# The first pair of an attention-and-FFN kernel worked by halves of heads, with another order of steps and loads

## The chip, the cores and the metric

The kernel runs on one core of one Trainium2 chip. The metric is the device time of one execution in microseconds, given as the median of several runs. The core's engines work side by side, each through its own queue in order: TensorE (products), VectorE, ScalarE, GpSimd (here almost only an issuer of loads) and SyncE (here an issuer of moves and stores). A trace of one profiled execution shows what each engine did and what it waited for.

## The reference

Attention in chunks of 64 tokens over 8 heads of 64, then a feed-forward part in which two products of the same input are multiplied element by element. Nothing stands between the last two weights, so the kernel multiplies them into one.

```python
# q, k, v: (8 batches, 8 heads, 576 tokens, 64), float32; chunks of 64 tokens
scores = scale * np.matmul(q_c, k_c.transpose(0, 1, 2, 4, 3))
scores = scores - np.max(scores, axis=-1, keepdims=True)
attn = np.exp(scores)
attn = attn / (np.sum(attn, axis=-1, keepdims=True) + 1e-09)
x = np.matmul(attn, v_c)          # then all heads side by side: (4608 tokens, 512)
a = x @ w1                        # w1, w2: (512, 1024)
b = x @ w2
out = (a * b @ w3) @ w_out        # w3: (1024, 1024), w_out: (1024, 512)
```

## The kernel before

The 4608 tokens are cut into 18 pairs of 256 tokens (four chunks, all heads). Two pairs make a group of 512 tokens. Every engine's work is written out by hand in one string, `ORDER`: a letter for the kind of step, then its pair (or group) and part. A loop calls the functions in that order, and `inorder` keeps each engine's instructions in the order of the string. So each engine, and GpSimd's queue of loads, works through its own letters of the string from left to right, and an instruction that waits holds up all that stands behind it on its engine.

The steps of pair p, with the line that the trace names:

- `R0`, `R1` load q and k of pair 0 as float32 by the queues of SyncE and ScalarE (L139); `K0`, `K1` cast them to bfloat16 on ScalarE (L145).
- `q`, `k`, `v` load the other pairs through GpSimd, which casts on the way (L99). `i0` to `i3` load a quarter of w1 and of w2 each, `o` loads w_out in four pieces, `h0` and `h1` load half of w3 in four pieces each. At most eight loads of GpSimd are under way: each further one waits for the landing of the one eight before it.
- `T p.0`, `T p.1` transpose q and k in blocks on VectorE (L205). `S p` is the scores on TensorE (L96), `E p` the exponential on ScalarE (L238), `P p` the product with v, which carries a column of ones for the sums (L96).
- `N p.0`, `N p.1` divide by the sums on VectorE (L266 and L269), `X p.0`, `X p.1` transpose the result into the input of the feed-forward part (L302, from pair 6 on L310).
- From pair 6 on, blocks are moved between partitions by DMAs of SyncE: `G` (four DMAs for each half) between T and S, `H` between X and A.
- `A p.j` and `B p.j` are x*w1 and x*w2 for a slice of the 1024 columns (L96; eight products of 256 columns up to pair 3, four products of 512 columns by groups after that). `C` copies A's result on ScalarE (L367), `M` multiplies it with B's on VectorE (L384).
- `V`, `W`, `Z` form w3*w_out once: transposes on VectorE (L425), products on TensorE, copies on ScalarE (L438).
- `O p` is the last product, 16 products of 512 columns (L96), `Y p` its copy on ScalarE (L414), `Q p` its store by SyncE.
- `D` are products of zeros on TensorE, into a PSUM tile that the next step will use: `D which.p.j.n.columns`.

PSUM is one pool of four tiles (two banks each) for scores, values, A with B, W and O. A tile comes free when its reader is through: E for scores, N for values, M for A and B, Z for W, Y for O. Tiles for q and k are five, for v six, for transposed q and k two (of a group each).

At the start TensorE runs 92 products of zeros with 16 columns and 8 with 512, then S0, P0, S1, five more products of zeros, and then the first x*w1, `A0.0`. Around `O0`, the first output product, the order before has `W3`, then `P4` and `S5`, then `O0`.

Of the kernel before, what the change touches and what calls it, by code (L numbers as in the profile page):

```python
# [24 lines left out]
G6.1 N10.1 C8.0 M6.7 M8.0 X10.0 X10.1 k15 P11 A8.1 A8.2 B8.1 N11.0 B8.2 k16 A8.3 C8.1 C8.2 N11.1
X11.0 B8.3 A8.4 M8.1 v13 B8.4 S12 C8.3 M8.2 S13 C8.4 H5.0 X11.1 M8.3 A8.5 E12 A8.6 C8.5 M8.4 B8.5
C8.6 T15.0 H5.1 B8.6 A8.7 B8.7 T15.1 M8.5 E13 P12 M8.6 A10.0 T16.0 B10.0 N12.0 C8.7 A10.1 N12.1 M8.7
P13 C10.0 v14 M10.0 C10.1 B10.1 N13.0 N13.1 A10.2 M10.1 X12.0 A10.3 B10.2 X12.1 C10.2 C10.3 q17
A10.4 M10.2 B10.3 x12 G7.0 B10.4 X13.0 G7.1 C10.4 A10.5 v15 k17 M10.3 X13.1 M10.4 x11 A10.6 S14 S15
T16.1 T17.0 T17.1 B10.5 C10.5 B10.6 C10.6 E14 O6 M10.5 Q5 M10.6 E15 P14 N14.0 N14.1 G8.0 Y6 X14.0 O7  # L30
# [17 lines left out]
def first_path(  # L48
# [46 lines left out]
    def mm(*a, **kw):
        return inorder(nc.tensor.matmul(*a, **kw))  # L96
# [34 lines left out]
    qk_t = {}  # L131

    HH = H // 2
    raw_t = {}
# [4 lines left out]
        inorder((nc.sync, nc.scalar)[s].dma_start(  # L139
            raw_t[s][:], (q, k)[s][0, :, 0:4 * CH, :].rearrange("h (p t) d -> p h (t d)", t=2)))  # L140

    def do_K(s):
# [2 lines left out]
        inorder(nc.scalar.copy(qk_t[0][:, s], raw_t[s][:]))  # L145
# [88 lines left out]

    def do_E(p, hh=None):
        if p not in e_t:
            e_t[p] = asb.tile([P, 2, H, CH], bf, tag="e", bufs=2, name="e")
        inorder(nc.scalar.activation(  # L238
            e_t[p][:, :, heads(hh)], s_t[p][:].rearrange("p u (h q) -> p u h q", q=CH)[:, :, heads(hh)],
            Exp, scale=scale, bias=0.0))  # L240
# [345 lines left out]
```

## Time and profile before

| | |
|---|---|
| median of 3 runs | 243.89 us (243.85 to 244.39) |
| profiled execution | 244.65 us, of it 243.1 from the first to the last instruction |
| TensorE busy | 229.1 us, 94% |
| VectorE, ScalarE, GpSimd busy | 152.9, 84.1, 83.9 us |
| mean granted TensorE clock | 0.985 |
| loads through GpSimd | 18.88 MB, 83.4% of the DMA engines' time |

A row of a timeline gives the start in microseconds from the span's start, the time that the row covers, the engine, the line, the operation with its output and inputs, how many instructions are merged, and in brackets the idle time of the engine before it with what ended it. A row of the table by stretches gives the stretch, its length, the busy time and instruction count of TensorE, of its weight load, of VectorE, ScalarE and GpSimd, then the granted clock, the mean number of tenths or share in which the DMA engines were busy, and GB/s. In the page's row of slices each digit is one fortieth of the span (6.1 us), in tenths. Ends of products are modelled, so a wait inside a group of products can hide in its busy time.

### The profile page before, as it was taken

The page shows a single profiled execution, that of the slowest core. Times are in us where ns is not written, and L with a number is a line of the kernel's source. Part 1 is how long each engine was busy: PE and PEld are TensorE (multiplying, and loading weights), DVE is VectorE, ACT ScalarE, POOL GpSimd, SP SyncE. Part 2 cuts the span into 40 slices and gives each one's busy share as a digit, 9 for nine tenths or more (in the row PEclk, how much of TensorE's full clock was granted, in tenths as well). Part 3 has the DMA queues.
Part 4 walks back from the last instruction along what each step waited for, and adds up shares of the span by engine and source line. Part 5 has one row for each costly group of instructions (what it writes and reads, how often), then busy time and mean ns, then how long its engine had stood idle before and what let it go on. Part 6 is the DMA issues. An engine that isn't in the chain of part 4 may idle for free.

```text
span 243.1 us, 6370 instructions
## 1 busy us (share of the span) xinstructions
PE 229.1 (94%) x2685; PEld 121.6 (50%) x2705; DVE 152.9 (63%) x235; ACT 84.1 (35%) x116; POOL 83.9 (35%) x114
## 2 busy tenths in 40 slices
PE   7479899999999899999999999999999999999994
PEld 5248778854545444443434444444444444444443
DVE  1678798789888598959878899663843422321200
ACT  2513423314422625333533435253224125323122
POOL 7757966656953353642920082000000000000000
PEclk9859999999999999999999999999999999999999
DMA  6999999999999999999999799647302142003234
GB/s 172 179 185 182 184 169 199 197 193 174 172 187 288 221 214 262 212 219 189 192 275 202 183 191 130 142 119 246 105 1 88 44 131 86 0 0 114 86 149 173
DMA packets 94366, 39.23 MB, mean 161 GB/s; under 512 B 75264, under 2 KB 86784, under 8 KB 94336
## 3 DMA queue, kind: packets, MB, share of 16 engines
q0 software_dynamic: 82592, 18.88, 83.4%
q1 hardware_dynamic: 10704, 19.41, 26.8%
q10 hardware_dynamic: 1040, 0.52, 0.8%
q8 instruction: 21, 0.34, 0.6%
q14 instruction: 9, 0.07, 0.1%
HBM read 38.80 MB, written 9.44 MB: 198 GB/s over the span
## 4 chain that ended last, share of the span: by engine, by line
PE 45%; DMA 41%; POOL 6%; DVE 3%; issue 3%; SPq 0%; POOLq 0%; DVEq 0%
PE ab_ps L96 27%; PE o_ps L96 17%; DMA qk<-in_k_dram 16%; DMA vbuf<-in_v_dram 12%; DMA w<-in_moe_w_dram 8%; DMA qkm<-qkT 3%; DMA xt<-xm 3%; POOL qk L99 2%; POOL vbuf L99 2%; POOL w L99 1%; DVE qkT L205 1%; POOL wo L99 1%; DVE xn L269 1%; PE pv L96 1%; DVE xm L310 1%
## 5 line engine op out<-in xcount | busy, mean ns | idle before, releaser
L96 PE MATMUL ab_ps<-xt,w 128*128 128x512 bf16 (+1 forms) x684 | 128.0, 342 | 2.2 <-DMA w<-in_moe_w_dram 0.6
L96 PEld LDWEIGHTS <-w 128*128 128x128 bf16 x704 | 67.0, 98 | 57.0 <-issue 2.3
L384 DVE TENSOR_TENSOR ab<-a_sb,ab_ps 128x512 bf16<-128x512 f32 x71 | 46.7, 674 | 47.2 <-PE ab_ps L96 40.4
L96 PE MATMUL o_ps<-w3o,ab 128*128 128x512 bf16 (+1 forms) x284 | 64.0, 373 | 0.8 <-DVE ab L384 0.2
L367 ACT COPY a_sb<-ab_ps 128x512 f32<-128x512 f32 x71 | 41.4, 588 | 67.0 <-PE ab_ps L96 61.5
L205 DVE STREAM_TRANSPOSE qkT<-qk 128x1024 bf16<-128x1024 bf16 x36 | 45.9, 1298 | 13.2 <-ACT qk L145 5.5
L96 PEld LDWEIGHTS <-ab 128*128 128x128 bf16 x296 | 28.5, 98 | 32.5 <-issue 0.2
L99 POOL DMA_DIRECT2D vbuf<-in_v_dram x40 | 33.9, 852 | 17.1 <-DMA qk<-in_k_dram 7.4
L414 ACT COPY o_sb<-o_ps 128x1024 f32<-128x1024 f32 x17 | 17.2, 1013 | 53.9 <-PE o_ps L96 44.4
L269 DVE TENSOR_TENSOR xn<-pv,rcs 128x512 bf16<-128x512 f32 x36 | 24.9, 691 | 1.3
L99 POOL DMA_DIRECT2D qk<-in_q_dram x23 | 18.1, 788 | 15.0 <-DMA qk<-in_q_dram 5.3
L238 ACT ACTIVATE e<-s_ps 128x1024 bf16<-128x1024 f32 x17 | 17.1, 1025 | 13.0 <-PE s_ps L96 12.8
L99 POOL DMA_DIRECT2D qk<-in_k_dram x23 | 18.1, 789 | 8.8 <-DMA vbuf<-in_v_dram 4.9
L310 DVE STREAM_TRANSPOSE xm<-xn 128x512 bf16<-128x512 bf16 x24 | 16.0, 689 | 0.1
L96 PE MATMUL w_ps<-wo,w3T 128*128 128x512 bf16 x62 | 13.9, 379 | 0.1
L266 DVE RECIPROCAL rcs<-pv 128x8 f32<-128x8 f32 x36 | 6.9, 192 | 10.6 <-PE pv L96 10.6
L99 POOL DMA_DIRECT2D w<-in_moe_w_dram x16 | 11.1, 696 | 5.5 <-DMA wo<-in_moe_w_out_dram 2.3
L96 PEld LDWEIGHTS <-e 64*32 64x32 bf16 (+1 forms) x768 | 7.6, 99 | 8.2 <-issue 5.1
L96 PE MATMUL pv<-vbuf,e 64*32 64x65 bf16 (+1 forms) x768 | 10.0, 198 | 1.7 <-ACT e L238 1.1
L425 DVE STREAM_TRANSPOSE w3T<-w 128x1024 bf16<-128x1024 bf16 x8 | 9.4, 1214 | 1.8 <-DMA w<-in_moe_w_dram 1.6
L96 PEld LDWEIGHTS <-w3T 128*128 128x128 bf16 x64 | 6.3, 98 | 7.3
L96 PE MATMUL z_ps<-zero 128*128 128x16 bf16 (+1 forms) x103 | 7.8, 222 | 1.9 <-DVE zero L115 1.4
(29 smaller groups left out, 48.9 us busy)
## 6 DMA issues: line engine op xcount, KB each, us to landing
out_dram<-o_sb SPq DMA_DIRECT2D x17, 512.0 KB, 3.4
qkm<-qkT SPq DMA_DIRECT2D x48, 128.0 KB, 6.5
vbuf<-in_v_dram POOLq DMA_DIRECT2D x32, 128.0 KB, 8.3
w<-in_moe_w_dram POOLq DMA_DIRECT2D x16, 256.0 KB, 9.5
xt<-xm SPq DMA_DIRECT2D x48, 64.0 KB, 3.7
qk<-in_q_dram POOLq DMA_DIRECT2D x11, 256.0 KB, 9.5
qk<-in_k_dram POOLq DMA_DIRECT2D x11, 256.0 KB, 10.6
wo<-in_moe_w_out_dram POOLq DMA_DIRECT2D x4, 256.0 KB, 7.1
```

The lines of the kernel that those rows point to most:

```text
L96: return inorder(nc.tensor.matmul(*a, **kw))
L99: return inorder(nc.gpsimd.dma_start(dst, src))
L205: inorder(nc.vector.transpose(qkT_t[g][:, :, p % 2, s, heads(h)].rearrange("p e h (y t) -> p h t e y", t=2), qk_t[p][:, s, heads(h)].rearr ...
L238: inorder(nc.scalar.activation(e_t[p][:, :, heads(hh)], s_t[p][:].rearrange("p u (h q) -> p u h q", q=CH)[:, :, heads(hh)], Exp, scale=sca ...
L266: inorder(nc.vector.reciprocal(rc, pv[:, :, :, D:W]))
L269: inorder(nc.vector.tensor_mul(xn_t[p][:, u], pv[:, :, :, 0:D], rc.to_broadcast([P, 2, 4, D])))
L310: inorder(nc.vector.transpose(xm_t[g][:, u, :, m].rearrange("p o (c y) -> p c o y", y=BL), xn_t[p][:].rearrange("p u r m d -> p (u r) m d" ...
L367: first[p, j] = inorder(nc.scalar.copy(a_t[p, j][:], ps_t[p, j][:, 0, :]))
L384: inorder(nc.vector.tensor_mul(o, view(a_t.pop((p, j))[:]), view(ps_t.pop((p, j))[:, 1, :])))
L414: inorder(nc.scalar.copy(o_sb[:], ps_t.pop(p)[:]))
L425: inorder(nc.vector.transpose(w3T_t[f][:].rearrange("p k (f y) -> p f k y", y=BL), w3[:, NB * f:NB * (f + 1), :].rearrange("p f (k x) -> p ...
```

## The change

`K`, `T`, `S`, `E` and `P` of pair 0 are each called twice, for heads 0 to 3 and 4 to 7. `K` learns to do half, and the scores of the two halves go to two PSUM tiles, so the first exponential need not wait for the second half's scores. The 92 small and 8 large products of zeros at the start become 16 large ones; six new ones stand in front of S1, and the five behind it become six. The whole string is in another order, for the steps and for the loads.

```diff
-R0 R1 v0 q1 k1 i0 v1 i1 i2 q2 k2 v2 i3 q3 k3 v3 q4 k4 v4 o h0 h1 D0.0.0.92.16 D0.0.0.8.512 K0 T0.0
-K1 T0.1 q5 k5 v5 S0 T1.0 E0 P0 T1.1 q6 k6 v6 N0.0 S1 D1.0.0.5.512 X0.0 N0.1 X0.1 A0.0 E1 B0.0 C0.0
...
-v7 V0 B3.2 C3.2 V1 A3.3 M3.2 S4 B3.3 W0 k9 C3.3 V2 V3 W1 Z0 V4 V5 T5.0 V6 V7 W2 Z1 W3 M3.3 T5.1 q10
-T6.0 E4 T6.1 Z2 P4 T7.0 S5 T7.1 N4.0 Z3 k10 O0 T8.0 O1 q11 E5 N4.1 X4.0 Y0 G3.0 q12 X4.1 Y1 k11 P5
-v8 N5.0 N5.1 O2 Q0 X5.0 X5.1 G3.1 A4.0 O3 T8.1 C4.0 Y2 S6 E6 S7 T9.0 T9.1 Q1 B4.0 T10.0 M4.0 A4.1
-G4.0 T10.1 E7 P6 Y3 B4.1 v9 N6.0 C4.1 N6.1 A4.2 G4.1 C4.2 B4.2 M4.1 X6.0 M4.2 A4.3 P7 q13 q14 N7.0
-Q2 B4.3 C4.3 A4.4 N7.1 k12 B4.4 M4.3 A4.5 X6.1 C4.4 C4.5 B4.5 A4.6 k13 k14 C4.6 M4.4 A4.7 S8 T11.0
-v10 B4.6 B4.7 M4.5 q15 X7.0 X7.1 M4.6 C4.7 S9 M4.7 E8 P8 N8.0 O4 E9 N8.1 Q3 P9 Y4 H3.0 O5 T11.1 X8.0
-T12.0 H3.1 v11 T12.1 Y5 N9.0 T13.0 A6.0 G5.0 B6.0 N9.1 X8.1 C6.0 X9.0 A6.1 C6.1 B6.1 T13.1 A6.2 B6.2
...
+R0 R1 v0 K0.0 T0.0.0 K0.1 K1.0 D0.0.1.16.512 T0.0.1 q1 K1.1 k1 T0.1.0 S0.0 T0.1.1 T1.0 S0.1 E0.0 i0
+E0.1 P0.0 P0.1 D0.1.0.6.512 N0.0 T1.1 S1 D1.0.0.6.512 E1 v1 i1 i2 N0.1 q2 X0.0 X0.1 k2 A0.0 P1 i3
+N1.0 v2 N1.1 B0.0 X1.0 X1.1 A0.1 C0.0 B0.1 C0.1 v3 A0.2 A1.0 M0.0 M0.1 B0.2 T2.0 B1.0 C0.2 C1.0 T2.1
...
+A1.3 X2.1 o B1.3 A2.0 T3.0 C1.2 C1.3 B2.0 T3.1 M1.2 C2.0 M1.3 q5 M2.0 S3 E3 A2.1 B2.1 C2.1 h1 T4.0
+q6 P3 A2.2 M2.1 q7 N3.0 N3.1 B2.2 A2.3 X3.0 C2.2 X3.1 C2.3 B2.3 T4.1 V0 A3.0 B3.0 M2.2 k5 C3.0 k6
+M2.3 V1 V2 A3.1 M3.0 k7 C3.1 B3.1 M3.1 V3 A3.2 T5.0 B3.2 W0 S4 Z0 V4 v4 V5 W1 V6 W2 E4 C3.2 Z1 V7 W3
+T5.1 Z2 q8 A3.3 T6.0 T6.1 T7.0 B3.3 T7.1 v5 Z3 M3.2 S5 C3.3 k8 M3.3 E5 T8.0 G3.0 O0 P4 N4.0 O1 q9
+N4.1 X4.0 q10 Y0 T8.1 G3.1 P5 X4.1 k9 N5.0 Y1 O2 Q0 X5.0 v6 S6 N5.1 X5.1 T9.0 T9.1 v7 S7 A4.0 Q1
+B4.0 E6 E7 O3 C4.0 M4.0 P6 N6.0 Y2 k10 N6.1 A4.1 C4.1 q11 v8 B4.1 G4.0 A4.2 Y3 C4.2 P7 v9 B4.2 M4.1
+k11 X6.0 X6.1 N7.0 A4.3 B4.3 N7.1 A4.4 A4.5 M4.2 T10.0 C4.3 G4.1 q12 B4.4 A4.6 M4.3 k12 C4.4 X7.0 Q2
+Q3 M4.4 H3.0 C4.5 S8 E8 T10.1 B4.5 X7.1 C4.6 M4.5 H3.1 B4.6 A4.7 M4.6 B4.7 C4.7 M4.7 P8 S9 E9 T11.0
+N8.0 O4 T11.1 Y4 O5 q13 N8.1 v10 T12.0 X8.0 X8.1 P9 A6.0 C6.0 N9.0 N9.1 T12.1 Y5 B6.0 A6.1 B6.1 C6.1
...
-    def do_K(s):
+    def do_K(s, h=None):
         if 0 not in qk_t:
             qk_t[0] = io.tile([P, 2, H, 2 * D], bf, tag="qk", bufs=5, name="qk")
-        inorder(nc.scalar.copy(qk_t[0][:, s], raw_t[s][:]))
+        inorder(nc.scalar.copy(qk_t[0][:, s, heads(h)], raw_t[s][:, heads(h)]))
...
     def do_S(p, hh=None):
         g, m = divmod(p, 2)
-        if p not in s_t:
-            s_t[p] = psum("s_ps")
+        if (p, hh) not in s_t:
+            s_t[p, hh] = psum("s_ps")
...
     def do_P(p, hh=None):
         e = e_t[p]
-        vb_free.append(vb_t[p])
+        if hh != 0:
+            vb_free.append(vb_t[p])
...
-        d, key = ((s_t, p), (ps_t, (p, j)), (pv_t, (p, 0)))[which]
+        d, key = ((s_t, (p, (None, 0)[j])), (ps_t, (p, j)), (pv_t, (p, 0)))[which]
```

More of the change, by code (lines that the diff above doesn't have):

```diff
@@ L25 @@
[L25 to L30, printed above, removed]
@@ new lines @@
+N8.0 O4 T11.1 Y4 O5 q13 N8.1 v10 T12.0 X8.0 X8.1 P9 A6.0 C6.0 N9.0 N9.1 T12.1 Y5 B6.0 A6.1 B6.1 C6.1
+A6.2 X9.0 B6.2 A6.3 G5.0 X9.1 M6.0 B6.3 A6.4 C6.2 B6.4 M6.1 G5.1 C6.3 T13.0 M6.2 k13 H4.0 A6.5 M6.3
+C6.4 q14 C6.5 S10 B6.5 v11 A6.6 H4.1 T13.1 E10 M6.4 P10 M6.5 S11 C6.6 B6.6 G6.0 N10.0 G6.1 q15 N10.1
+k14 A6.7 v12 M6.6 X10.0 E11 P11 B6.7 A8.0 N11.0 k15 C6.7 B8.0 A8.1 C8.0 q16 k16 X10.1 M6.7 N11.1
+B8.1 T14.0 A8.2 C8.1 A8.3 B8.2 C8.2 M8.0 M8.1 B8.3 X11.0 Q4 S12 S13 C8.3 M8.2 v13 X11.1 T14.1 H5.0
@@ new lines @@
+A8.4 E12 C8.4 B8.4 M8.3 A8.5 E13 P12 M8.4 N12.0 A8.6 C8.5 B8.5 q17 N12.1 A8.7 C8.6 M8.5 T15.0 k17
+x12 T15.1 B8.6 X12.0 B8.7 T16.0 v14 O6 C8.7 T16.1 M8.6 v15 H5.1 A10.0 M8.7 Y6 B10.0 Q5 C10.0 A10.1
+C10.1 M10.0 P13 N13.0 G7.0 A10.2 T17.0 B10.1 B10.2 v16 C10.2 x11 N13.1 A10.3 A10.4 C10.3 B10.3 M10.1
+A10.5 T17.1 C10.4 G7.1 M10.2 B10.4 B10.5 S14 M10.3 C10.5 G8.0 M10.4 X12.1 X13.0 G8.1 E14 S15 H6.0
+X13.1 O7 M10.5 P14 N14.0 E15 A10.6 N14.1 Y7 B10.6 A10.7 C10.6 Q6 M10.6 P15 N15.0 C10.7 S16 N15.1
+X14.0 B10.7 H6.1 M10.7 O8 A12.0 X14.1 E16 B12.0 C12.0 A12.1 Q7 Y8 X15.0 X15.1 P16 v17 M12.0 S17
@@ new lines @@
+N16.0 B12.1 H7.0 A12.2 C12.1 B12.2 M12.1 E17 C12.2 P17 N16.1 H7.1 A12.3 B12.3 N17.0 M12.2 A12.4
+B12.4 A12.5 C12.3 B12.5 M12.3 N17.1 C12.4 A12.6 X16.0 M12.4 C12.5 A12.7 C12.6 B12.6 M12.5 A14.0
+C12.7 Q8 O9 M12.6 A14.1 Y9 B12.7 C14.0 B14.0 M12.7 B14.1 A14.2 C14.1 B14.2 A14.3 X16.1 M14.0 C14.2
+M14.1 A14.4 B14.3 X17.0 C14.3 O10 Y10 M14.2 A14.5 M14.3 C14.4 A14.6 C14.5 B14.4 B14.5 C14.6 B14.6
+H8.0 A14.7 Q9 M14.4 O11 Q10 B14.7 Y11 X17.1 H8.1 C14.7 M14.5 M14.6 A16.0 A16.1 A16.2 M14.7 C16.0
+B16.0 Q11 M16.0 B16.1 A16.3 O12 C16.1 C16.2 Y12 B16.2 M16.1 A16.4 B16.3 A16.5 M16.2 C16.3 C16.4
@@ L40 @@
+B16.4 B16.5 O13 M16.3 C16.5 M16.4 A16.6 Q12 A16.7 Y13 Q13 M16.5 B16.6 O14 C16.6 B16.7 M16.6 C16.7
+O15 M16.7 Y14 Q14 O16 Y15 Q15 Y16 Q16 O17
 """
@@ L140, in do_R, with heads @@
             raw_t[s][:], (q, k)[s][0, :, 0:4 * CH, :].rearrange("h (p t) d -> p h (t d)", t=2)))
-    def do_K(s):
+    def heads(h):
+        return slice(0, H) if h is None else slice(h * HH, (h + 1) * HH)
+    def do_K(s, h=None):
         if 0 not in qk_t:
             qk_t[0] = io.tile([P, 2, H, 2 * D], bf, tag="qk", bufs=5, name="qk")
-        inorder(nc.scalar.copy(qk_t[0][:, s], raw_t[s][:]))
-    def heads(h):
-        return slice(0, H) if h is None else slice(h * HH, (h + 1) * HH)
+        inorder(nc.scalar.copy(qk_t[0][:, s, heads(h)], raw_t[s][:, heads(h)]))
     def load_qk(p, which, h=None):
@@ L225, in do_S @@
                     for i in range(NB):
-                        mm(s_t[p][half[i % 2], i // 2, h * CH:(h + 1) * CH],
+                        mm(s_t[p, hh][half[i % 2], i // 2, h * CH:(h + 1) * CH],
                            lhsT=qkT_t[g][blk[i], e, m, 1, h, :], rhs=qkT_t[g][blk[i], e, m, 0, h, :],
@@ L230, in do_S @@
                 for i in (0, 3, 1, 2):
-                    mm(s_t[p][half[i % 2], i // 2, h * CH:(h + 1) * CH],
+                    mm(s_t[p, hh][half[i % 2], i // 2, h * CH:(h + 1) * CH],
                        lhsT=qkm_t[g][half[i // 2], i % 2, m, 1, h, :],
@@ L238, in do_E @@
         inorder(nc.scalar.activation(
-            e_t[p][:, :, heads(hh)], s_t[p][:].rearrange("p u (h q) -> p u h q", q=CH)[:, :, heads(hh)],
+            e_t[p][:, :, heads(hh)], s_t[p, hh][:].rearrange("p u (h q) -> p u h q", q=CH)[:, :, heads(hh)],
             Exp, scale=scale, bias=0.0))
```

16 lines of the change are left out of this document (1 added, 15 removed).

## The prediction

> **What bounds the kernel now.** I read the page first (busy shares, clock, queues), then TensorE's timeline for the stretches where it should be dense and is not, then the timelines of the engines it waits for.
>
> ```profile
> PE 229.1 (94%) x2685; PEld 121.6 (50%) x2705; DVE 152.9 (63%) x235; ACT 84.1 (35%) x116; POOL 83.9 (35%) x114
> PEclk9859999999999999999999999999999999999999
> DMA  6999999999999999999999799647302142003234
> GB/s 172 179 185 182 184 169 199 197 193 174 172 187 288 221 214 262 212 219 189 192 275 202 183 191 130 142 119 246 105 1 88 44 131 86 0 0 114 86 149 173
> ```
>
> TensorE is the bound at 94%, and the work that it must do does not change. So the change can only move the time in which it waits: in the first 17 us, and in the first 140 us where the DMA engines are full (9 in every slice) and the loads can be late. The wait list names few waits of TensorE, but many hide inside groups. I therefore price its steps in a stretch without waits and count what is missing elsewhere.
>
> ```profile
> 174.00:235.00 61.00, 60.79 (x280) 27.68 (x283) 17.07 (x26) 18.03 (x27) 0.00 (x0) 1.00 0.19 64
> 78.00 3.62 PE L96 MATMUL o_ps<-w3o,ab 128*128 128x512 bf16 x16
> 102.69 3.63 PE L96 MATMUL o_ps<-w3o,ab 128*128 128x512 bf16 x15
> 120.14 0.45 PE L96 MATMUL pv<-vbuf,e 64*64 64x65 bf16 x32
> 120.42 0.46 PE L96 MATMUL s_ps<-qkm 64*64 64x64 bf16 x32
> 120.81 1.04 PE L96 MATMUL ab_ps<-xt,w 128*128 128x512 bf16 x4
> 122.40 1.89 PE L96 MATMUL ab_ps<-xt,w 128*128 128x512 bf16 x8 [0.55 <-DMA qkm<-qkT]
> 124.22 0.45 PE L96 MATMUL pv<-vbuf,e 64*64 64x65 bf16 x32
> 124.60 7.08 PE L96 MATMUL ab_ps<-xt,w 128*128 128x512 bf16 x32
> 138.16 0.45 PE L96 MATMUL pv<-vbuf,e 64*64 64x65 bf16 x32
> ```
>
> From 174 to 235 the program has 282 products of 512 columns: 61.00 / 282 = 0.216 us each. A lone visit to attention (S or P) costs 124.60 - 124.22 = 0.38, and 122.40 to 124.22 is 0.09 more than 8 products: 0.47. A visit of two blocks costs 120.81 - 120.14 + 0.09 = 0.76.
> From O3 (78.00) to O5 (102.69) the order has 15 A or B steps of 4 products and two O steps of 16: 92 x 0.216 = 19.9, plus 4 lone and 2 double visits, 3.4: 23.3 of 24.69 us, so 1.4 us is lost. From O5 to P12 (138.16): 144 products, 31.15, plus 2 lone and 2 double visits, 2.5: 33.6 of 35.47, so 1.85 us is lost. In sum 3.25 us. Its causes stand on VectorE:
>
> ```profile
> 80.70 1.33 DVE L205 STREAM_TRANSPOSE qkT<-qk 128x1024 bf16<-128x1024 bf16 x1 [1.80 <-DMA qk<-in_k_dram]
> 83.03 1.32 DVE L205 STREAM_TRANSPOSE qkT<-qk 128x1024 bf16<-128x1024 bf16 x1 [1.00 <-DMA qk<-in_q_dram]
> 105.78 1.33 DVE L205 STREAM_TRANSPOSE qkT<-qk 128x1024 bf16<-128x1024 bf16 x1 [2.38 <-DMA qk<-in_k_dram]
> 98.77 3.61 PE L96 MATMUL o_ps<-w3o,ab 128*128 128x512 bf16 x15 [0.21 <-DVE ab L384]
> ```
>
> By the order these are T9.1, T10.0 and T12.1. Behind T12.1 stands N9.0, whose PSUM tile A6.1 and A6.2 need; behind T10.0 stand M4.0 and N6. VectorE waits 5.2 us in the three and TensorE loses about 2.9 of it (0.35 of the 3.25 belongs to O4, 98.77, which waits for a product on VectorE).
>
> **The change: the front.** The halves of pair 0 go from cast to values.
>
> ```profile
> 6.19 2.02 ACT L145 CAST qk<-raw 128x1024 bf16<-128x1024 f32 x2 [3.42 <-DMA raw<-in_q_dram]
> 7.27 2.48 DVE L205 STREAM_TRANSPOSE qkT<-qk 128x1024 bf16<-128x1024 bf16 x2 [5.47 <-ACT qk L145]
> 10.57 1.02 ACT L238 ACTIVATE e<-z_ps 128x1024 bf16<-128x1024 f32 x1 [2.36 <-PE z_ps L96]
> 10.83 1.32 DVE L205 STREAM_TRANSPOSE qkT<-qk 128x1024 bf16<-128x1024 bf16 x1 [1.09 <-DMA qk<-in_q_dram]
> 16.00 0.71 DVE L302 STREAM_TRANSPOSE xt<-xn 128x512 bf16<-128x512 bf16 x1
> 4.29 3.05 PE L96 MATMUL z_ps<-zero 128*128 128x512 bf16 x7 [0.23 <-issue]
> 16.77 2.17 PE L96 MATMUL z_ps<-xt,w 128*128 128x256 bf16 x16
> 26.76 0.70 PE L96 MATMUL s_ps<-qkT 32*64 32x64 bf16 x64
> 28.05 1.05 PE L96 MATMUL ab_ps<-xt,w 128*128 128x256 bf16 x8 [0.59 <-DMA w<-in_moe_w_dram]
> 25.39 1.32 DVE L205 STREAM_TRANSPOSE qkT<-qk 128x1024 bf16<-128x1024 bf16 x1 [0.52 <-DMA qk<-in_k_dram]
> ```
>
> No row shows a cast, transpose or exponential of half a tile. Their bounds: half of the whole one (0.51, 0.62, 0.51) and all of it (1.02, 1.25, 1.02). I take 0.55, 0.65 and 0.6, near the 0.71 that the 128x512 transpose at 16.00 takes. Then S0 starts at about 8.8 instead of 9.80 and P0 ends near 10.8. But VectorE cannot begin T1.0 before q1 lands (10.83), the load queue up to k2 being the same. From there it has the same 1.3 + 1.3 + 2 x 0.9 + 2 x 0.65 us to X0.1, and ends at 16.5 (16.71 before). With halves at their upper bound P0 ends at 12.6 and X0.1 at 17.0. The front of pair 0 is worth -0.2 to +0.3 at the first x*w1.
> Zero products: 3.05 / 7 = 0.43 each at half clock, so 16 end by 8.3, before S0. The six in front of S1 end by 13.5, before T1.1 (14.3). The six behind S1 (one more) end at 16.4 at full clock, at 17.5 at half: up to 0.75 later than 16.77.
> All of this is covered: S2 (26.76) waits for k2, whose transpose starts at 25.39 in both. The last quarter of w1 is loaded before v2 now, so the 0.59 at 28.05 goes; v2 and k3 come some 3 us later and take it back at P2 and S3. What ends last in this stage is VectorE ahead of O0:
>
> ```profile
> L99 POOL DMA_DIRECT2D w<-in_moe_w_dram x6: 642/645/645, 38.1 to 44.0; - x6
> DMA to landing us min/median/max: 10.0/10.2/10.4
> 54.62 2.37 DVE L425 STREAM_TRANSPOSE w3T<-w 128x1024 bf16<-128x1024 bf16 x2 [0.23 <-PE w_ps L96]
> 60.34 0.65 DVE L384 TENSOR_TENSOR ab<-a_sb,ab_ps 128x512 bf16<-128x512 f32 x1
> 60.91 3.65 DVE L205 STREAM_TRANSPOSE qkT<-qk 128x1024 bf16<-128x1024 bf16 x3
> 64.75 0.70 PE L96 MATMUL pv<-vbuf,e 64*32 64x65 bf16 x64
> 65.37 0.71 PE L96 MATMUL s_ps<-qkT 32*64 32x64 bf16 x64
> 66.01 7.08 PE L96 MATMUL o_ps<-w3o,ab 128*128 128x512 bf16 x31
> ```
>
> The last piece of h1 lands at 44.0 + 10.4 = 54.4 before, and at about 54.1 after (q5 is in front of it in place of v4, two pieces). Behind it the new order has V4 to V7 (1.19 each), T5.1, T6.0, T6.1, T7.0, T7.1 (1.22 each) and M3.2 (0.65), whose PSUM tile O0 takes: 54.15 + 4.75 + 6.1 + 0.65 = 65.65. O0 starts then instead of 66.01, but P4 (65.37 - 64.75 = 0.62, with the change of shape 0.75) stood before O0 and now stands behind it: -0.36 + 0.75 = **+0.4**. TensorE, without P4, is ready at about 66.01 - 0.75 = 65.25, so 0.4 us of front delay costs nothing; beyond that each us costs one.
>
> **The change: the middle.** The margins named here are estimates: the new order laid out step by step with the prices above, a load landing behind the one in front of it. T9.1: k9 is issued ahead of v6 and v7 but behind q10. A 256 KB piece is 262 / 185 GB/s = 1.4 us (an estimate by the page's GB/s row), so k9 is 1.4 us earlier, and the wait of 1.80 nearly goes. T10.0 now stands behind N6, N7 and M4.2, some 7 us of TensorE's work later: its 1.00 goes. k12 is issued ahead of q13 and q14, 2.8 us earlier, and T12.1 stands behind N9.0 and N9.1: its 2.38 goes. The moves G3 start at T7.1's end, some 2.5 us earlier on SP's queue; v6 and v7 keep about 3 us before P6 and P7. So of 2.9 us all could go. I keep 0.35 at O4, 0.2 for one more visit (28 against 27) and 0.6 for new waits where the margins are thin, T11.1 and T12.0 with under 2 us. **-2.9 + 0.2 + 0.6 = -2.1.** From O9 on both orders run dense.
>
> **Sum.** +0.4 - 2.1 = -1.7 us. The profiled execution took 244.65 (span 243.1), which gives 242.95. The runs without it have a median of 243.89, 0.76 less; if that is fewer late loads, the gain there is -0.95, if not -1.7. I take -1.4: **242.5 us**.
>
> [...] Loads and moves slow each other:
>
> ```profile
> DMA to landing us min/median/max: 7.4/7.4/7.6
> DMA to landing us min/median/max: 16.1/16.5/18.0
> ```
>
> Loads of q and k issued at 24 to 31 us land after 7.4 us; those issued at 66 to 76, beside SP's moves, after 16.5. [...]
>
> **Rivals.**
> 1. Slower: the load stream runs later than laid out, because the moves start earlier and share it. The new order still has T9.1, T11.1 and T12.0 in line ahead of N and M steps with 0.9, 1.8 and 1.6 us to spare. 5 us late, VectorE waits 4.1 + 3.3 = 7.4 us; by the ratio above (2.9 of 5.2) TensorE loses 4.1 instead of 2.9. With +0.4 and 0.2 that is +1.8: 245.7. It ends slower from about 4 us on. For it: 16.5 us to landing. Against: k9, k10 and k12 all stand earlier. Chance 0.15.
> 2. Half: k9 stays late and a G move takes the place of another wait; 1.5 us of the 2.9 stays: 243.7. Chance 0.15.
> 3. The clock. The granted clock falls after the first pause:
>
> ```profile
> 12.00:16.00 4.00, 2.52 (x112) 1.71 (x100) 3.72 (x7) 1.02 (x1) 2.11 (x3) 0.50 1.86 179
> 16.00:18.00 2.00, 2.00 (x12) 1.25 (x11) 0.71 (x1) 0.00 (x0) 1.36 (x3) 0.68 1.46 196
> ```
>
> It is at half from 12 at the latest to 17.3 (0.68 over the two us from 16). [...] If the pause before S1 holds it down for half as long again, 2.6 us more, TensorE reaches O0 1.3 us later, less 0.4 of cover: +0.9, so 243.4. Chance 0.06.
>
> The main case has 0.64, with 241.4 to 243.2 of its own. 0.3% (0.73 us) is about what this measurement tells from no change. Faster: 0.64, same: 0.21 (rivals 2 and 3), slower: 0.15. The range 241.4 to 244.2 leaves out rival 1 and a little below.
>
> **What would show it.** Right: P0 ends before 11; first x*w1 at 16.5 to 17.5; S2 still near 26.7; O0 near 65.6 behind M3.2 with P4 after it; no wait for a load over 1 us on VectorE from 78 to 110, and O3 to P12 without 3 us lost. Wrong: O0 after 66.5, or load waits there of 4 us in sum.

## The result, and the profile after

| | before | after |
|---|---|---|
| median of 17 runs each, on one chip | 244.75 us (243.85 to 245.59) | 242.09 us (241.83 to 243.94) |
| ratio after / before, 95% interval | | 0.9899 (0.9883 to 0.9914) |
| profiled execution, its span | 244.65, 243.1 us | 242.01, 240.5 us |

The kernel after is 1.0% faster, about 2.5 us; 1.4 us had been forecast, from the median of three earlier runs. In later comparisons the kernel before had medians of 244.1 to 244.6 us, so each variant below is given as a ratio to the runs of before beside it.

The page of the kernel after (busy shares, then the granted clock and the DMA engines' busy share in 40 slices):

```profile
PE 230.6 (96%) x2608; PEld 120.2 (50%) x2628; DVE 152.2 (63%) x237; ACT 84.2 (35%) x119; POOL 83.8 (35%) x114
PEclk9889999999999999999999999999999999999999
DMA  6999999999999999999999999663200422120234
```

TensorE does the same work, but for 77 zero products fewer, in a shorter span. The table by stretches and TensorE's timeline show the front:

```profile
10.00:12.00 2.00, 1.72 (x65) 1.14 (x67) 1.97 (x4) 0.60 (x1) 1.19 (x2) 0.55 1.57 191
12.00:14.00 2.00, 1.96 (x32) 0.68 (x34) 1.97 (x5) 0.00 (x0) 0.90 (x2) 0.60 1.80 188
14.00:16.00 2.00, 1.95 (x68) 1.23 (x58) 1.27 (x3) 1.02 (x1) 0.78 (x1) 1.00 1.95 172
```

```profile
1.44 6.25 PE L97 MATMUL z_ps<-zero 128*128 128x512 bf16 x16 [1.44 <-DVE zero L116]
8.89 0.44 PE L97 MATMUL z_ps<-qkT 32*64 32x64 bf16 x32 [1.21 <-DVE qkT L206]
10.05 1.23 PE L97 MATMUL pv<-vbuf,e 64*32 64x65 bf16 x64
15.72 1.16 PE L97 MATMUL z_ps<-xt,w 128*128 128x256 bf16 x8
26.29 0.71 PE L97 MATMUL s_ps<-qkT 32*64 32x64 bf16 x64 [0.32 <-DVE qkT L206]
65.56 3.61 PE L97 MATMUL o_ps<-w3o,ab 128*128 128x512 bf16 x15 [0.33 <-DVE ab L386]
69.10 0.70 PE L97 MATMUL pv<-vbuf,e 64*32 64x65 bf16 x64
73.29 0.72 PE L97 MATMUL pv<-vbuf,e 64*32 64x65 bf16 x64
```

S0 starts at 8.89 (before 9.80), the first x*w1 at 15.72 (16.77), S2 at 26.29 (26.76), O0 at 65.56 (66.01), with P4 behind it, and P5 at 73.29. The clock is back to full by 14 us instead of 17.3. VectorE's timeline, ahead of O0 and at the first load that it waits for:

```profile
9.83 1.32 DVE L206 STREAM_TRANSPOSE qkT<-qk 128x1024 bf16<-128x1024 bf16 x1 [0.39 <-DMA qk<-in_q_dram]
54.46 4.62 DVE L427 STREAM_TRANSPOSE w3T<-w 128x1024 bf16<-128x1024 bf16 x4 [2.96 <-DMA w<-in_moe_w_dram]
59.00 5.95 DVE L206 STREAM_TRANSPOSE qkT<-qk 128x1024 bf16<-128x1024 bf16 x5
64.86 1.24 DVE L386 TENSOR_TENSOR ab<-a_sb,ab_ps 128x512 bf16<-128x512 f32 x2
```

In the middle the waits of VectorE for loads are gone: its timeline has none behind the one at 54.46. TensorE's timeline there (the last two rows are O6 and A10.0):

```profile
79.88 3.62 PE L97 MATMUL o_ps<-w3o,ab 128*128 128x512 bf16 x16
97.88 7.07 PE L97 MATMUL o_ps<-w3o,ab 128*128 128x512 bf16 x31 [0.18 <-DVE ab L386]
131.34 0.45 PE L97 MATMUL pv<-vbuf,e 64*64 64x65 bf16 x32
136.05 3.62 PE L97 MATMUL o_ps<-w3o,ab 128*128 128x512 bf16 x15
139.50 2.75 PE L97 MATMUL ab_ps<-xt,w 128*128 128x512 bf16 x12
```

From O3 (79.88) to P12 (131.34) are 51.46 us. The order after has 212 products of 512 columns there (45.86 at the prediction's 0.216), six lone visits (0.47) and three double ones (0.76): 50.96. It loses 0.5 us where before lost 3.25.

By stretches of the two profiled executions (starts of steps on TensorE):

| | before | after | difference |
|---|---|---|---|
| up to P5 | 73.02 | 73.29 | +0.27 |
| P5 to A6.0 | 33.14 | 32.12 | -1.02 |
| A6.0 to A10.0, less O6 (3.45), which after has in it | 32.56 | 30.64 | -1.92 |
| A10.0 to O17, less O6, which before has in it | 94.00 | 94.03 | +0.03 |

### The profile page after: what moved, and what is told of

Its sections match the earlier page's. It is cut to its first block, busy times and chain, and to the rows that moved or that the text cites. A ratio compares the mean times of both kernels' runs of the same rounds, so it can differ in the third digit from the quotient of the medians.

```text
span 240.5 us, 6230 instructions
## 1 busy us (share of the span) xinstructions
PE 230.6 (96%) x2608; PEld 120.2 (50%) x2628; DVE 152.2 (63%) x237; ACT 84.2 (35%) x119; POOL 83.8 (35%) x114
## 4 chain that ended last, share of the span: by engine, by line
PE 71%; DMA 18%; DVE 4%; POOL 3%; issue 2%; DVEq 0%; POOLq 0%
PE ab_ps L97 41%; PE o_ps L97 26%; DMA w<-in_moe_w_dram 9%; DMA qk<-in_k_dram 6%; DMA wo<-in_moe_w_out_dram 3%; PE pv L97 2%; DVE qkT L206 2%; POOL vbuf L100 2%; PE s_ps L97 2%; DVE w3T L427 1%; POOL qk L100 1%; DVE ab L386 1%; DVE o_sb L409 0%; DVEq L427 0%; DVEq L206 0%
## 5 line engine op out<-in xcount | busy, mean ns | idle before, releaser
L206 DVE STREAM_TRANSPOSE qkT<-qk 128x1024 bf16<-128x1024 bf16 (+1 forms) x38 | 45.9, 1235 | 8.2 <-ACT qk L149 5.1
L416 ACT COPY o_sb<-o_ps 128x1024 f32<-128x1024 f32 x17 | 17.3, 1015 | 50.1 <-PE o_ps L97 50.1
L239 ACT ACTIVATE e<-s_ps 128x1024 bf16<-128x1024 f32 (+1 forms) x17 | 16.8, 999 | 14.1 <-PE s_ps L97 13.9
L97 PE MATMUL z_ps<-zero 128*128 128x512 bf16 x26 | 10.1, 545 | 1.7 <-DVE zero L116 1.4
```

What stands on the lines that cost most here:

```text
L206: inorder(nc.vector.transpose(qkT_t[g][:, :, p % 2, s, heads(h)].rearrange("p e h (y t) -> p h t e y", t=2), qk_t[p][:, s, heads(h)].rearr ...
L239: inorder(nc.scalar.activation(e_t[p][:, :, heads(hh)], s_t[p, hh][:].rearrange("p u (h q) -> p u h q", q=CH)[:, :, heads(hh)], Exp, scale ...
L416: inorder(nc.scalar.copy(o_sb[:], ps_t.pop(p)[:]))
```

## Experiments

The theory: the gain is made in the middle by the order of steps and loads, and the front is covered. Rivals: the front (halves, zero products, clock) makes it; or an edit in the middle only moves a wait.

### Old front, new order behind it

```diff
 A1.0 A1.1 B1.0 T2.0 T2.1 q7 B1.1 S2
-M0.2 C1.0 C1.1 A0.3 E2 M1.0 P2 k7 B0.3 M1.1 A1.2 N2.0
+C1.0 M0.2 A0.3 M1.0 C1.1 E2 B0.3 P2 C0.3 M1.1 A1.2 M0.3 N2.0
...
```

> The kernel before up to S2 (whole tiles for pair 0, 92 small and 8 large zero products, the loads up to q7 in the old order), and behind S2 what is left in the order of the kernel after. Theory (the gain is made in the middle, the front is covered by S2's wait for k2 and VectorE's work ahead of O0): 242.1 to 242.8 us, 0.8 to 1.1% faster than before; the first x*w1 back at about 16.8, but O0 within 0.5 us of 65.6 and no wait for a load over 1 us on VectorE from 78 to 110 but perhaps T9.1's. Rival (the halves, the zero products and the shorter time at half clock made the gain): 244 us or more, within 0.4% of before.

Measured: 247.85 us, ratio 1.0135 (1.0108 to 1.0162): slower than before. VectorE and TensorE in its timelines, and one stretch of its table:

```profile
49.09 1.25 DVE L425 STREAM_TRANSPOSE w3T<-w 128x1024 bf16<-128x1024 bf16 x1 [4.46 <-DMA w<-in_moe_w_dram]
50.97 3.57 PE L96 MATMUL ab_ps<-xt,w 128*128 128x256 bf16 x16 [3.44 <-DVE ab L384]
50.00:53.00 3.00, 2.03 (x10) 1.43 (x10) 3.00 (x5) 0.59 (x1) 1.50 (x3) 0.50 1.46 194
```

The new order has V0 right behind T4.1 and ahead of M2.2. With the old loads, where h0 stands behind v4 and o, V0 waits 4.46 us, M2.2 with it, and TensorE 3.44. With the wait the granted clock falls: it is at half (0.50 in the row) from 49.8 to 56.6 us, so some 5.7 us of TensorE's work behind the wait run at half speed (0.22 us for each of the 16 products in the row, 0.11 for the 64 at 19.50 us in before), an estimated 2.8 us more. P5 starts at 80.25, 7 us late; this profile is the slowest of the six runs. From there to O17 it takes 160.30 us, as after does (160.25) and not as before (163.15). So the time met neither theory nor rival: the middle's gain does not need the new front, but the new order of steps up to O0 needs its own order of loads.

### New front, old order behind it

```diff
 T2.0 B1.0 C0.2 C1.0 T2.1 A1.1 B1.1 M0.2 S2
-A0.3 M1.0 q3 C1.1 E2 B0.3 P2 k3 q4 C0.3 h0 k4 M1.1
+q3 k3 q4 k4 v4 o h0 h1 q5 k5 v5 q6 k6
...
```

> The reverse: the kernel after up to S2 (halves of heads, 16 + 6 + 6 zero products, the new order of the loads up to v3), and behind S2 what is left in the order of before. Theory: within 0.3% of before (244.0 to 244.9 us), the waits of VectorE for k9, q10 and k12 in T9.1, T10.0 and T12.1 still there with 4 to 6 us in sum, although the first x*w1 starts about 1 us earlier. Rival (the front made the gain): 242 to 243 us.

Measured: 244.09 us, ratio 1.0000 (0.9984 to 1.0015). TensorE's timeline, then VectorE's:

```profile
15.07 0.49 PE L97 MATMUL z_ps<-xt,w 128*128 128x256 bf16 x3
72.80 0.72 PE L97 MATMUL pv<-vbuf,e 64*32 64x65 bf16 x64
```

```profile
83.57 1.32 DVE L206 STREAM_TRANSPOSE qkT<-qk 128x1024 bf16<-128x1024 bf16 x1 [3.71 <-DMA qk<-in_q_dram]
105.25 1.31 DVE L206 STREAM_TRANSPOSE qkT<-qk 128x1024 bf16<-128x1024 bf16 x1 [1.65 <-DMA qk<-in_k_dram]
```

The first x*w1 starts 1.7 us earlier than before, P5 only 0.2, and the late loads of the middle are still there with 5.4 us. With the old order the new front is worth nothing: the rival falls.

### Three transposes later, one load earlier

```diff
-S6 E6 S7 T9.0 T9.1 Q1 B4.0 T10.0 M4.0 A4.1
-G4.0 T10.1 E7 P6
+S6 E6 S7 T9.0 T9.1 Q1 B4.0 M4.0 A4.1
+G4.0 E7 P6
...
+k12
 q13 q14 N7.0
-Q2 B4.3 C4.3 A4.4 N7.1 k12 B4.4
+Q2 B4.3 C4.3 A4.4 N7.1 T10.0 T10.1 B4.4
...
-T12.0 H3.1 v11 T12.1 Y5 N9.0 T13.0 A6.0 G5.0 B6.0 N9.1
+T12.0 H3.1 v11 Y5 N9.0 A6.0 G5.0 B6.0 N9.1 T12.1 T13.0
```

> The kernel before with five tokens moved: T10.0 and T10.1 stand behind N7.1, T12.1 and T13.0 behind N9.1, and k12 is issued ahead of q13 and q14. Theory (TensorE's loss between O3 and P12 comes from those two places, 2.9 us for 5.2 us of VectorE's waits): T10.0's 1.00 and T12.1's 2.38 go, T9.1's 1.80 stays, so 3.4 x 0.56 = 1.9 us: 242.6 to 243.3 us, 0.6 to 0.9% faster. Rival (the loads as a whole are late, so the wait only moves to the next transpose): within 0.3% of before.

Measured: 244.83 us, ratio 1.0045 (1.0020 to 1.0071), no gain. The timeline of TensorE, and that of SyncE's queue with the moves H3, first of this kernel, then of before, then of after:

```profile
108.13 8.15 PE L96 MATMUL ab_ps<-xt,w 128*128 128x512 bf16 x37 [1.95 <-DMA xt<-xm]
```

```profile
96.83 5.40 SPq L197 DMA_DIRECT2D xt<-xm  x8
```

```profile
95.43 4.97 SPq L197 DMA_DIRECT2D xt<-xm  x8
```

```profile
92.39 5.25 SPq L198 DMA_DIRECT2D xt<-xm  x8
```

Both waits went, and O3 to S8 took 0.74 us less, A6.0 to A10.0 1.75 less. T9.1's wait, which was to stay, is 2.05. But the two T10 steps now stand ahead of X7.0 and X7.1, so the moves H3 start 1.4 us later and A6.0 waits 1.95 for them. The wait moved from a load to a move, as the rival had it. In after H3 starts at 92.39.

### The same with the moves kept in time, and the loads alone

Relative to the run before this one:

```diff
-Q2 B4.3 C4.3 A4.4 N7.1 T10.0 T10.1 B4.4
+Q2 B4.3 C4.3 A4.4 N7.1 T10.0 B4.4
...
-C4.6 M4.4 A4.7 S8 T11.0 v10 B4.6 B4.7 M4.5 q15 X7.0 X7.1 M4.6 C4.7 S9 M4.7 E8
+C4.6 M4.4 A4.7 S8 v10 B4.6 B4.7 M4.5 X7.0 X7.1 T10.1 M4.6 C4.7 S9 M4.7 T11.0 q15 E8
```

> The kernel before with the order of VectorE's steps mended in the middle: T10.0 behind N7.1, T10.1 behind X7.1, T11.0 behind M4.7, so that X7.0 and X7.1 and the moves H3 behind them start no later than in before; T12.1 and T13.0 behind N9.1; k12 issued ahead of q13 and q14. In the earlier run with both T10 steps ahead of X7 the first stretch gained 0.74 us and the second 1.75, and a wait of TensorE for H3's moves of 1.95 took them back. Theory (the gain of the middle is the order of the transposes behind late loads, as long as the moves start in time): both gains stay, TensorE waits under 0.5 us for the moves at A6.0: 2.0 to 2.5 us less than before, 241.7 to 242.4 us. Rival (what is gained in the one place is lost in the next, whatever the order): within 0.3% of before.

The other edit moves no step of before, only loads:

```diff
-v7 V0 B3.2 C3.2 V1 A3.3 M3.2 S4 B3.3 W0 k9
+V0 B3.2 C3.2 V1 A3.3 M3.2 S4 B3.3 W0 k9
...
-Z3 k10 O0
+Z3 k10 v7 O0
...
-q13 q14 N7.0 Q2 B4.3 C4.3 A4.4 N7.1 k12
+k12 q13 q14 N7.0 Q2 B4.3 C4.3 A4.4 N7.1
```

> The kernel before with no step moved and three loads in another order: v7 behind k10 instead of ahead of k9, and k12 ahead of q13 and q14. By the landings of before k9, q10 and k10 land 1.75 us earlier and k12 2.8 us earlier. Theory (VectorE's waits for these loads are the loss, by 0.56 us of TensorE's time for each us of wait): T9.1's 1.80 and T12.1's 2.38 go, T10.0 keeps up to 1.0 behind the earlier T9.1: 4.2 of 5.2 us, 2.3 us less than before, 241.7 to 242.5 us. Rival (the load order is worth nothing by itself, since v7, q13 or q14 are late in turn): within 0.3% of before.

Measured: 243.36 us, ratio 0.9968 (0.9944 to 0.9992), for the steps; 243.46 us, ratio 0.9965 (0.9942 to 0.9989), for the loads: 0.8 us each, not 2.0 to 2.5, and hardly outside the rival's 0.3%. TensorE's timeline, first of the one, then of the other:

```profile
137.49 2.75 PE L96 MATMUL ab_ps<-xt,w 128*128 128x512 bf16 x12 [0.94 <-DMA qkm<-qkT]
```

```profile
137.37 2.75 PE L96 MATMUL ab_ps<-xt,w 128*128 128x512 bf16 x12 [1.50 <-DMA qkm<-qkT]
```

VectorE's waits for loads from 78 to 110 us shrank from 5.2 to 0.82 and 1.06 (with the loads alone, T10.0 waits 1.34 for moves instead), and TensorE came to P12 2.1 and 2.7 us earlier than before (136.10 and 135.43 against 138.16). Behind it the products of A10 then wait 0.94 and 1.50 for SyncE's moves, which before had hidden. (The rows name the moves that stand behind H5 in SyncE's queue; by the order A10.0 reads what H5 brings, begun at 127.23 and 126.55.) In after O6 stands there, 3.6 us of products ahead of A10.0 (the row at 136.05 above).

### Both mends, and O6 ahead of A10.0

```diff
-M8.6 A10.0 T16.0 B10.0 N12.0 C8.7 A10.1 N12.1 M8.7
+M8.6 O6 A10.0 T16.0 B10.0 N12.0 C8.7 A10.1 N12.1 M8.7 Y6
...
-B10.6 C10.6 E14 O6 M10.5 Q5
+B10.6 C10.6 E14 M10.5 Q5
...
-N14.0 N14.1 G8.0 Y6 X14.0 O7
+N14.0 N14.1 G8.0 X14.0 O7
```

> The kernel before with the two mends of its middle together (the transposes behind the late loads moved as in the run on VectorE's order; v7 behind k10 and k12 ahead of q13 and q14) and O6 with Y6 moved ahead of A10.0, where TensorE waited 0.9 and 1.5 us for H5's moves in the two runs with one mend. The front stays that of before. Theory (three causes in a row: late loads, VectorE's order, and moves that the faster TensorE then meets; after cured all): no wait for a load over 0.6 us on VectorE from 78 to 110, no wait of TensorE over 0.5 us for moves from 100 to 145, 2.0 to 3.0 us less than before, 241.2 to 242.2 us. Rival (another wait takes their place again): 243.2 to 243.8, as each mend alone.

Measured: 246.76 us, ratio 1.0100 (1.0068 to 1.0132). Both cures came as meant (no wait of VectorE for a load from 78 to 110 us, none of TensorE for moves over 0.38 from 100 to 145), and from P5 to A10.0, less O6, the kernel takes 1.6 us less than before. But other waits came, as the rival had it, and they cost more than the rival's price:

```profile
168.59 2.75 PE L96 MATMUL ab_ps<-xt,w 128*128 128x512 bf16 x12 [0.89 <-DMA xt<-xm]
172.58 0.32 PE L96 MATMUL pv<-vbuf,e 64*64 64x65 bf16 x16 [0.89 <-DVE ab L384]
```

O6 is missing where it stood: from A10.0 to O17 it takes 97.33 us where 94.0 would do without O6, with waits of 0.73, 0.29, 0.89 and 0.89 us from 156 to 173. The stretch up to P5 is also 1.4 us longer (74.41), with pauses of TensorE of 0.73 and 0.79 us that no edit there explains; what they are comes below. This profile is the slowest of the six runs.

### P4 ahead of O0 in the kernel after

```diff
-T5.1 Z2 q8 A3.3 T6.0 T6.1 T7.0 B3.3 T7.1 v5 Z3 M3.2 S5 C3.3 k8 M3.3 E5 T8.0 G3.0 O0 P4 N4.0 O1
+T5.1 Z2 q8 A3.3 T6.0 T6.1 T7.0 B3.3 T7.1 v5 Z3 M3.2 P4 S5 C3.3 k8 M3.3 E5 T8.0 G3.0 O0 N4.0 O1
```

> The kernel after with one token moved: P4 stands ahead of S5, so ahead of O0 as in before. Theory (my front term: O0 is set by M3.2 on VectorE, TensorE waits 0.33 us for it, and P4 with its change of shape costs 0.75 behind O0): 0.33 of the 0.75 is hidden, O0 starts at about 65.95 and everything behind P4's old place is 0.3 to 0.4 us earlier: 241.6 to 241.8 us, 1.2% faster than before. Rival (P4's place is worth nothing, since what follows is set by loads or VectorE): the same as after, 242.0 to 242.2.

Measured: 242.26 us, ratio 0.9921 (0.9906 to 0.9936), as after or a little behind it.

```profile
65.62 0.32 PE L97 MATMUL pv<-vbuf,e 64*32 64x65 bf16 x32 [0.75 <-DVE ab L386]
66.54 7.08 PE L97 MATMUL o_ps<-w3o,ab 128*128 128x512 bf16 x31
```

P4's second half needs a PSUM tile too, and gets it from M3.2 on VectorE: it waits the 0.75 us that was to be saved. P4's place costs nothing (P5 starts at 73.55, in after at 73.29): the same VectorE step frees the tile for whoever comes first.

### Pieces of three orders together

```diff
-N4.1 X4.0 q10 Y0 T8.1 G3.1 P5 X4.1 k9 N5.0 Y1 O2 Q0 X5.0
+N4.1 X4.0 Y0 G3.0 q12 X4.1 Y1 k11 P5 T8.1 G3.1 N5.0 O2 Q0 X5.0
```

> Three pieces put together: the kernel after up to S2, then the order of before up to P5 (with P4 ahead of O0, and k9 issued ahead of v7), then what is left in the order of after. The new front with before's steps reached P5 at 72.80 us, after at 73.28, and after needs 160.0 us from P5 to its last output product. Theory (stages add up if the loads stay in time): 0.3 to 0.5 us less than after, 241.5 to 241.9 us. Rival (after's order behind P5 leans on its own loads and moves, as the old front with the new order did): a new wait of over 1 us, 243 us or more.

Measured: 248.05 us, ratio 1.0133 (1.0092 to 1.0174).

```profile
80.66 0.91 PE L97 MATMUL s_ps<-qkm 64*64 64x64 bf16 x63 [2.70 <-DMA qkm<-qkT]
81.50:84.80 3.30, 3.30 (x16) 1.19 (x9) 0.00 (x0) 3.24 (x4) 0.88 (x1) 0.50 1.40 289
```

The new order has O2 alone between P5 and S6 on TensorE; S6 reads what the moves G3 bring, and the old order up to P5 issues them later: SyncE begins them at 67.95 us, in after at 64.98. S6 waits 0.79 and 2.70 us, and behind it the granted clock is at half for 3.4 us (0.50 in the second row). The rival, at another place than I thought.

### The front undone in the kernel after

First all of it, then the zero products alone, then the halves alone; the order of steps and loads stays.

```diff
-R0 R1 v0 K0.0 T0.0.0 K0.1 K1.0 D0.0.1.16.512 T0.0.1 q1 K1.1 k1 T0.1.0 S0.0 T0.1.1 T1.0 S0.1 E0.0 i0
-E0.1 P0.0 P0.1 D0.1.0.6.512 N0.0 T1.1 S1 D1.0.0.6.512 E1
+R0 R1 v0 K0 D0.0.0.92.16 D0.0.0.8.512 T0.0 q1 K1 k1 T0.1 T1.0 S0 i0
+E0 P0 N0.0 T1.1 S1 D1.0.0.5.512 E1
```

> The kernel after with its front undone but its order of loads and of all other steps kept: whole tiles for pair 0 from cast to values, 92 zero products of 16 columns and 8 of 512 at the start, none in front of S1, five behind it. Theory (the front is covered by S2's wait and VectorE's work ahead of O0): the first x*w1 0.8 to 1.5 us later than in after, S2 within 0.5 us of 26.3, O0 within 0.3 us of 65.2 to 65.6, and the time that of after within 0.4 us: 241.8 to 242.5 us, 0.8 to 1.1% faster than before. Rival (halves and zero products bring the gain): 243.3 us or more.

```diff
-D0.0.1.16.512
+D0.0.1.92.16 D0.0.1.8.512
```

> The kernel after with one thing undone: its 16 zero products of 512 columns at the start are the 92 of 16 columns and 8 of 512 of before again; halves of heads, the six products in front of S1 and the order stay. With the whole front undone the time was 0.53% under before instead of 1.0%, and in that profile TensorE was at half clock for 10.24 us, up to 20.6, and S2 waited 2.0 us for VectorE. Theory (the halves bring P0's values 1.6 us earlier and with them VectorE's N and X steps and T2.1; that is what the front is worth): 242.0 to 242.4 us, 0.8 to 1.1% faster than before. Rival (the zero products hold the clock, and the clock is the front's worth): 242.9 to 243.5 us with two or three stretches of 3.41 us at half clock.

```diff
-R0 R1 v0 K0.0 T0.0.0 K0.1 K1.0 D0.0.1.16.512 T0.0.1 q1 K1.1 k1 T0.1.0 S0.0 T0.1.1 T1.0 S0.1 E0.0 i0
-E0.1 P0.0 P0.1 D0.1.0.6.512 N0.0 T1.1 S1 D1.0.0.6.512 E1
+R0 R1 v0 K0 D0.0.0.16.512 T0.0 q1 K1 k1 T0.1 T1.0 S0 i0
+E0 P0 D0.1.0.6.512 N0.0 T1.1 S1 D1.0.0.6.512 E1
```

> The kernel after with the other thing undone: whole tiles for pair 0 from cast to values; the 16 zero products, the six in front of S1 and the order stay. Theory (halves): P0 ends near 12.5 and S2 is 1 to 2 us later than 26.3: 242.8 to 243.4 us, 0.4 to 0.7% faster than before. Rival (clock): 242.0 to 242.5 us, with S2 within 0.5 us of 26.3.

Measured: 243.22 us, ratio 0.9947 (0.9922 to 0.9973), with all undone; 242.84 us, 0.9943 (0.9919 to 0.9966), with the old zero products; 242.87 us, 0.9938 (0.9918 to 0.9958), with whole tiles. (The 2.0 us named for S2 in the second expectation stood at S1 in that trace.) Each loses about half of the gain, and both together no more than one. For whole tiles that is what the theory had, with S2 1.2 us later than in after (27.48). All undone lies between its theory and its rival. The old zero products cost about what their rival named, but with one stretch of 3.4 us at half clock and not two or three. TensorE's timelines, in that order:

```profile
28.27 0.71 PE L96 MATMUL s_ps<-qkT 32*64 32x64 bf16 x64
34.75 3.22 PE L96 MATMUL ab_ps<-xt,w 128*128 128x256 bf16 x28 [1.00 <-issue]
```

```profile
32.18 3.00 PE L97 MATMUL ab_ps<-xt,w 128*128 128x256 bf16 x26 [0.93 <-issue]
77.31 1.24 PE L97 MATMUL o_ps<-w3o,ab 128*128 128x512 bf16 x5 [0.64 <-issue]
```

```profile
18.25 0.71 PE L96 MATMUL z_ps<-xt,w 128*128 128x256 bf16 x5 [0.85 <-issue]
31.56 0.31 PE L96 MATMUL pv<-vbuf,e 64*32 64x65 bf16 x31 [1.18 <-issue]
```

Two things show. In after TensorE reaches O0 only 0.33 us before VectorE (the row at 65.56), so a longer delay of TensorE in the first 65 us is no longer covered, as it still is in the old order: O0 starts at 67.06 with all undone and at 66.38 with whole tiles, and O17 is 1.5 and 1.0 us later than in after. With the old zero products O0 starts at 65.73, so what delays TensorE ahead of it is covered; there the loss stands behind O0, most of it from P5 to O3 (0.8 us), where the pause inside O2 lies. And a part of the delay are pauses put down to issue, 1.2 to 2.0 us in sum, at the same counts of TensorE's instructions from kernel to kernel; after has 0.22 and 0.16, at other counts. They are not all of it: with all undone S2 is 2.0 us late ahead of any such pause, with the clock at half up to 20.6 us.

How much of each loss is pause stays open, for each is read from one profiled execution. Up to 47 us the kernel before and four of its variants (three transposes later, the same with the moves in time, the loads alone, both mends) are the same program, and at one and the same count their pauses are 0.37, 0.55, 0.35, none and 0.73 us.

### As many zero products as before, in another mix

```diff
-D0.0.1.16.512
+D0.0.1.10.512 D0.0.1.90.16
```

> The kernel after with its 16 zero products at the start replaced by 10 of 512 columns and 90 of 16: about as long in sum, large ones first, and as many products (100) as with the old zero products. The run with the old ones lost TensorE 0.93 us inside B1.2 and 0.64 inside O2, put down to issue, while the granted clock and the start of S0 were as in after. Such pauses stand at the same counts of TensorE's instructions from kernel to kernel (before and its variants at 1215 to 1217, others at 449, 961 and 2497, which are 256 or multiples of it apart), so 84 more products move other steps onto them. Theory (the count of instructions made the loss, not the clock): the pauses are back at the same counts, over 0.3 us in sum, and the time is that of the run with the old zero products, 242.5 to 243.1 us. Rival (the columns of the zero products matter, through the clock): 241.9 to 242.3 us, as after.

Measured: 244.28 us, ratio 0.9991 (0.9972 to 1.0009): the whole gain is gone, more than expected.

```profile
13.60 0.26 PE L97 MATMUL pv<-vbuf,e 64*32 64x65 bf16 x5 [2.24 <-issue]
34.44 0.81 PE L97 MATMUL ab_ps<-xt,w 128*128 128x256 bf16 x6 [1.54 <-issue]
```

The pauses stand at 449 and 1217 of TensorE's instructions, and a third of 0.36 at 2497: 4.1 us, of which 2.3 arrive at the end (O17 at 235.84 against 233.53). In this mix eighty-four more small products cost as much as the change brings; in the mix of the old zero products, of the same number, they cost half. So the number alone is not the cause, as the theory had it; the last section shows what differs. In this profile the clock was also at half for longer (its mean was 0.985 against 0.993), so the two are not quite apart; but the pauses are idle time, not slow products.

No variant beat the kernel after.

## Why the prediction was right or wrong

The time, 242.09 us, lies in the range and 0.4 below the forecast, and the cause named as the likeliest is the one that the stretches show. That it lies so near is in part luck: the forecast started from 243.89, which the 17 runs put at 244.75, and took 1.4 off where about 2.5 came, so that two errors cancel.

- **S0 and P0.** S0 at 8.89, forecast 8.8. Casts, transposes and exponentials of half a tile took 0.55, 0.64 and 0.60 us (taken at 0.55, 0.65, 0.6). The 16 zero products took 0.39 us each and ended at 7.69, forecast 0.43 and 8.3. That they run "at half clock" is read from their time alone, about twice 0.216: the record of the granted clock begins at 7.1 us in before and at 6.8 in after. P0 ended at 11.28, so the sign "P0 ends before 11" failed: it fell into the stretch at half clock (0.55 from 10 to 12).
- **The first x*w1, 16.5 to 17.5.** Wrong: 15.72. The step that failed is "VectorE cannot begin T1.0 before q1 lands (10.83), the load queue up to k2 being the same". The queue is the same, but q1 landed 1 us earlier (T1.0 at 9.83); the last section says with what that goes.
- **O0.** Right: 65.56 against 65.65, from h1's landing at 54.46, four V steps, five transposes and M3.2. P4 with its change of shape took 0.72, forecast 0.75 (from O0 to P5 7.73 us with it, 7.01 in before without). But P4's place is not what costs there (the run with P4 ahead); up to P5 the order costs 0.27, forecast 0.4.
- **Covered front.** Right for the two kernels compared (the new front with the old order gains nothing), but the margin is thin: in the new order 0.4 us of cover was forecast and 0.33 stands there, and any one part of the front undone costs about 1 us. So the gain stands on the front too: with all of it undone 0.53% is left, and with ten and ninety zero products nothing. S2 was not set by k2, as the prediction had it: VectorE begins T2.0 at 23.46, when q2 lands, k2's transpose follows without a wait, and S2 starts at 26.29.
- **The middle.** The sum was right: 2.9 us to be had, 2.75 came from O3 to P12. It goes with the order behind P5 and not with the front: from P5 to O17 after and the kernels that share that order take 160.2 to 161.4 us with six fronts (the run of pieces, whose S6 waits, apart), before 163.15 and the new front with the old order 163.7. But "2.9 of 5.2 us of VectorE's waits" is not a price at which each wait can be bought: one mend alone gave 0.8 us, because TensorE then came to the moves too early. The new order also has H3 3 us earlier (92.39 against 95.43) and O6 ahead of A10.0, which the prediction did not count as part of the gain. What each of these is worth no run shows alone.
- **The allowance of 0.6 for new waits** was not needed: none of VectorE's waits behind 54.46 us is for a load. That, and 0.2, is the term mis-sized in the sum, -1.7 where the profiles show -2.6.
- **The last 0.3**, taken off because three runs of before had a median 0.76 under its profiled execution, was wrong: 17 runs have 244.75, and later sets of runs 244.1 to 244.6.
- **Bandwidth.** Another order of loads alone brought 0.35%. From 70 to 140 us the DMA engines move 222 GB/s in before and 225 in after, the last number in the tables by stretches, first of before, then of after:

```profile
70.00:140.00 70.00, 67.85 (x814) 31.73 (x820) 56.96 (x88) 27.55 (x39) 26.27 (x33) 1.00 1.55 222
```

```profile
70.00:140.00 70.00, 69.20 (x827) 32.77 (x834) 59.48 (x92) 27.04 (x39) 32.59 (x44) 1.00 1.65 225
```

- **Rivals.** Rival 1 (the load stream runs late because moves share it) did not come. That loads and moves slow each other is a reading of the profile of before: SyncE's moves of 128 KB have a median of 7.3 us to landing from 60 to 80 us, where GpSimd's queue moves 2.52 MB, and of 2.3 from 150 to 200, where it moves 0.15. No run changed one of the two alone. Late loads or moves did make two of the mixed orders slower, by 1.35 and 1.33%, but through their place in the order. Rival 2 (k9 late) did not come either. Rival 3 (the clock) went the other way: half clock lasts 3.4 us in after and 6.8 in before. In one profile each, the kernels with six zero products in front of S1 are at half clock for none to 3.4 us (6.8 with ten and ninety, behind a pause of 2.24), those without for 6.8 to 10.2; no run took the six away alone.

## What to carry to other kernels

Price a stall at what ends next behind it, not at its own length: with four queues in a row (loads, VectorE, moves, TensorE) curing late loads alone gave a third of the sum (0.8 of 2.5 us). The order that gave all of it also starts moves earlier and keeps a block of independent products for the place where they land. Look at the clock around a long wait of TensorE: in the two runs where it waited 3.4 and 3.5 us the clock was at half for 6.8 and 3.4 us. Take an order of steps and its order of loads as one thing; of three mixes of the two orders, two were slower than both and one as slow as the slower. And do not take small products for free: here eighty-four more of them cost half of the gain in one mix and all of it in another.
